# The last three chunks of an MLP weight brought by four loads of 32 partitions with an outermost dimension of eight

## The chip, the cores and the metric

The kernel runs on one core of one Trainium2 chip. The metric is the device time of one execution in microseconds (us). Three runs of the kernel before took 393.94, 395.52 and 395.59 us; their median is 395.52 us. One more execution was profiled, and all views of the profile are of that one.

## The reference, cut to what matters

A decode step for a batch of 8, one token each, in float32: adaptive layer norm, attention over the last 2048 rows of a cache of 8 key/value heads, and an MLP with squared ReLU. The lines that this case touches are the MLP's:

```python
mod = (_silu(c) @ w_mod).reshape(c.shape[0], 6, 1, -1)
sa, ca, ga, sb, cb, gb = (mod[:, i] for i in range(6))
x = x + ga * attention(layernorm(x) * (1 + ca) + sa, k_cache, v_cache, wq, wo)
h = layernorm(x) * (1 + cb) + sb
h = h @ w1 + b1                    # 512 -> 1792
r = jnp.where(h > 0, h, 0)
out = (r * r) @ w2 + b2            # 1792 -> 512
x = x + gb * out
```

## The kernel before, in words

Everything big is read once from HBM. Four SBUF slots of 4 MB (`slot0` to `slot3`, 128 partitions by 32 KB) take turns. `loads` is a list written out by hand: two halves of `w_mod`, two of `wq`, then key and value tiles of each batch element, two parts of `wo`, then `w1`, then `w2`. `pump()` issues the next loads as soon as a slot is free, all on SyncE's queue (SP); `done()` gives a slot back after its last matmul and pumps again. A large load has 128 partitions outermost, and its rows of HBM are split over the 16 DMA engines.

`w2` (1792 rows by 512) lies in its slot so that partition p holds rows 14p to 14p+13; "chunk" c (0 to 13) is row 14p+c of every partition, 256 KB over the 128 partitions. Before, `load` (L71 to L99) brings the chunks by four loads: 0 to 7, 8 to 11, 12, and 13. Since a later load on SP takes the semaphore of the one eight loads earlier, it is issued only after that one has landed.

The tail of the kernel is a chain. Matmuls with `wo` (L453) follow the two last `wo` loads; their output is added up (L463 to L471), normed, scaled and turned (`h2T`), and multiplied by `w1` (L485). ScalarE takes the ReLU into `r` (L493), VectorE squares it (L494). `r` has 128 partitions (four groups of 32, one per quarter of the 1792 hidden columns; the batch of 8 lies in the first rows of each group) by 448 columns. `to_columns` (L142, called at L496) turns 32x32 blocks of `r` into `rT`, 128 partitions by 14 chunks by 32, so that partition p of chunk c holds hidden column 14p+c. The 14 chunks are then multiplied by the chunks of `w2` in order (L505): four matmuls for each chunk, one per quarter of the output, each of which appears twice in the trace (112 entries). Two VectorE operations (L513, L514) make the output `y`, which SP stores (L515).

Of the kernel before, what the change touches and what calls it, by code (L numbers as in the profile page):

```python
# [18 lines left out]
def tile_adaln_cached_attention_mlp(  # L19
# [14 lines left out]
    nc = tc.nc  # L34
    P = 128
    B, HKV, SK, DH = k_cache.shape
    D = wq.shape[0]
# [33 lines left out]
    def load(key):  # L71
        s = free.pop(0)
        t = slots[s]
        held[key] = s
        kind = key[0]
        if kind in "KV":

            src = k_cache if kind == "K" else v_cache
            v = src[key[1], 4 * key[2] : 4 * key[2] + 4, SK - W :, :]
            v = v.rearrange("x (i j) d -> i x (j d)", i=32)  # L80
            nc.sync.dma_start(t, v)
            return
        if kind == "mod":
            pieces = [(0, w_mod.rearrange(r_kc, p=P)[:, 2 * key[1] : 2 * key[1] + 2])]
        elif kind == "wq":
            pieces = [(0, wq.rearrange(r_kc, p=P)[:, 2 * key[1] : 2 * key[1] + 2])]
        elif kind == "wo":
            v = wo.rearrange("(p i) n -> p i n", p=P)
            cuts = ((0, 16),) if key[1] == 0 else ((16, 28), (28, 32))
            pieces = [(lo - 16 * key[1], v[:, lo:hi]) for lo, hi in cuts]  # L90
        elif kind == "w1":
            v = w1.rearrange(r_kc, p=P)
            pieces = [(0, v[:, :2]), (2, v[:, 2:])]
        else:
            v = w2.rearrange("(p c) n -> p c n", p=P)
            pieces = [(lo, v[:, lo:hi]) for lo, hi in ((0, 8), (8, 12), (12, 13), (13, 14))]
        for lo, v in pieces:
            a, n = v.shape[1:]
            nc.sync.dma_start(t[:, lo * n : (lo + a) * n].rearrange("p (a n) -> p a n", n=n), v)  # L99

    def slot(key, n):
        t = slots[held[key]]
        return t[:, : t.shape[1] // n * n].rearrange("p (a n) -> p a n", n=n)
# [11 lines left out]
    def pump():  # L115
        while at[0] < len(loads) and free:
            load(loads[at[0]])
            at[0] += 1
# [22 lines left out]
    def to_columns(t, dest):  # L141
        nc.vector.transpose(dest, t.rearrange("p (l c) -> p c l", l=32))  # L142
# [349 lines left out]
    r = work.tile([P, FG], F32, name="relu", tag="a")  # L492
    nc.scalar.activation(r, ph[:, :FG], AF.Relu)  # L493
    nc.vector.tensor_mul(r, r, r)  # L494
    rT = work.tile([P, FC, 32], F32, name="rT", bufs=1)
    to_columns(r, rT)  # L496

    py = ps_t.tile([P, 512], F32, name="t_ps")
    for q in range(NQ):
# [52 lines left out]
```

## Time and profile before

| what | value |
|---|---|
| median of three runs | 395.52 us |
| the profiled execution's own time | 395.58 us |
| its span, first to last instruction | 393.7 us |
| PE / DVE / ACT busy, share of the span | 66% / 54% / 11% |
| 16 DMA engines, mean rate over the span | 419 GB/s |
| last `w2` matmul group (L505) | 112 entries, 4.9 us |
| `rT` transpose before it | 1 operation, 942 ns |

The profile is of one execution. Its own time, 395.58 us, is 1.9 us above the span, which counts only from the first to the last instruction. Most of the span is bound by the transfers (the DMA row of the 40 slices stands at 9 tenths from the second slice to the last but one); the change sits in the last 10 us.

### The profile page before, as it was taken

The numbers are of one execution on the slowest core, as the hardware profiler recorded it, in microseconds if no ns is written. First come the engines' busy times: TensorE is split into PE (matmuls) and PEld (weight loads), VectorE is DVE, ScalarE is ACT, GpSimd is POOL, SyncE is SP. The second block draws the span as 40 slices with busy tenths as digits, with TensorE's granted clock in tenths as the row PEclk, the third lists the DMA queues.
The fourth block names the chain that finished last, engine by engine and source line by source line (L and its number), as shares of the span: only waits on it lengthen the run. The fifth ranks groups of instructions, "written<-read, shape, count | busy, mean of one in ns | idle before, by whom it ended". The sixth has DMA issues, their size and how long they took to land.

```text
span 393.7 us, 4788 instructions
## 1 busy us (share of the span) xinstructions
PE 258.6 (66%) x2128; PEld 114.7 (29%) x2128; DVE 213.5 (54%) x226; ACT 42.0 (11%) x87; POOL 4.7 (1%) x12
## 2 busy tenths in 40 slices
PE   0445808678966694949394939393949394884784
PEld 0211301151441343324232523142215231451124
DVE  2420299399394849284928491849284926320022
ACT  1300100030030012001200120012001200130010
POOL 4000000000000000000000000000000000000000
PEclk9986758969975986889777968896779588998968
DMA  8999999999999999999999999999999999999992
GB/s 330 430 429 431 443 433 429 436 429 426 424 429 431 433 431 436 433 428 428 429 429 424 439 429 439 429 421 433 431 433 428 434 426 431 433 428 426 415 421 109
DMA packets 6853, 165.15 MB, mean 419 GB/s; under 512 B 808, under 2 KB 1072, under 8 KB 1328
## 3 DMA queue, kind: packets, MB, share of 16 engines
q1 hardware_dynamic: 6624, 164.69, 97.7%
q8 instruction: 17, 0.28, 0.3%
q10 hardware_dynamic: 144, 0.13, 0.1%
q14 instruction: 4, 0.03, 0.0%
q0 software_dynamic: 64, 0.01, 0.0%
HBM read 164.77 MB, written 0.07 MB: 419 GB/s over the span
## 4 chain that ended last, share of the span: by engine, by line
DMA 52%; PE 23%; DVE 22%; ACT 1%; issue 1%; DVEq 0%; ACTq 0%
DMA slot<-in_A_k_cache_dram 43%; DVE slot L287 20%; PE s_ps L297 15%; DMA slot<-in_A_wo_dram 7%; DMA xc_in<-in_xc_dram 3%; PE m_ps L221 2%; PE t_ps L485 1%; PE t_ps L505 1%; PE s_ps L453 1%; PE o_ps L378 1%; PE t_ps L366 1%; DVE pT L367 0%; PE t_ps L480 0%; PE m_ps L167 0%; ACT sq L163 0%
## 5 line engine op out<-in xcount | busy, mean ns | idle before, releaser
L287 DVE STREAM_TRANSPOSE slot<-slot 128x2048 f32<-128x2048 f32 x64 | 144.0, 2283 | 43.5 <-DMA slot<-in_A_k_cache_dram 43.3
L297 PE MATMUL s_ps<-slot,qb 128*32 128x512 f32 x512 | 121.1, 1095 | 69.6 <-DVE slot L287 68.7
L297 PEld LDWEIGHTS s_ps<-slot,qb 128*32 128x32 f32 x512 | 23.3, 136 | 147.0 <-issue 80.2
L378 PE MATMUL o_ps<-slot,pT 128*32 128x256 f32 x1024 | 59.6, 380 | 1.0 <-DMA slot<-in_A_v_cache_dram 1.0
L378 PEld LDWEIGHTS o_ps<-slot,pT 128*32 128x32 f32 x1024 | 47.0, 112 | 27.6 <-issue 18.2
L366 PE MATMUL t_ps<-ident,prd 128*128 128x128 f32 x128 | 27.4, 376 | 16.7 <-ACT prd L356 9.8
L309 DVE STREAM_TRANSPOSE s<-s_ps 128x512 f32<-128x512 f32 x8 | 5.7, 717 | 54.2 <-PE s_ps L297 54.2
L366 PEld LDWEIGHTS t_ps<-ident,prd 128*128 128x128 f32 x128 | 20.6, 192 | 22.3 <-ACT prd L356 22.1
L356 ACT ACTIVATE prd<-pr,rz 128x512 f32<-128x512 f32 x32 | 20.5, 710 | 9.6 <-DVE rz L348 9.6
L332 ACT ACTIVATE pr<-s,nm 128x512 f32<-128x512 f32 x8 | 5.8, 722 | 142.6 <-DVE nm L326 142.6
L367 DVE TENSOR_TENSOR pT<-t_ps,m 128x512 f32<-128x512 f32 x32 | 20.2, 668 | 0.7 <-PE t_ps L366 0.6
L388 ACT COPY o_sb<-o_ps 128x256 f32<-128x256 f32 x16 | 5.8, 363 | 121.9 <-PE o_ps L378 121.9
L243 PE MATMUL t_ps<-slot,h1T 128*32 128x512 f32 x64 | 12.5, 950 | 9.4 <-DMA slot<-in_A_wq_dram 9.4
L453 PE MATMUL s_ps<-slot,oT 128*32 128x512 f32 x64 | 8.9, 704 | 7.1 <-DMA slot<-in_A_wo_dram 7.1
L255 DVE STREAM_TRANSPOSE qT<-t_ps 128x512 f32<-128x512 f32 x2 | 1.4, 716 | 19.1 <-PE t_ps L243 18.9
L274 DVE TENSOR_TENSOR qb<-qrep,block 128x512 f32<-128x512 f32 x8 | 8.8, 1097 | 2.2 <-ACT qrep L266 2.2
L158 PE MATMUL m_ps<-xsum,sel 128*128 128x1 f32 x2 | 0.6, 363 | 14.0 <-DVE xsum L181 14.0
L344 PE MATMUL m_ps<-z,same 128*128 128x1 f32 x16 | 3.3, 273 | 9.2 <-ACT pr L332 9.2
L463 DVE COPY at_i<-s_ps 128x256 f32<-128x256 f32 x1 | 0.4, 424 | 15.3 <-PE s_ps L453 15.3
L243 PEld LDWEIGHTS t_ps<-slot,h1T 128*32 128x32 f32 x64 | 2.9, 163 | 18.8 <-issue 13.3
L221 PE MATMUL m_ps<-slot,cT 128*32 128x384 f32 x64 | 7.5, 639 | 0.0
L404 DVE TENSOR_TENSOR og<-m_ps,m 128x128 f32<-128x128 f32 x8 | 2.2, 271 | 9.1 <-PE m_ps L396 9.1
(91 smaller groups left out, 96.2 us busy)
## 6 DMA issues: line engine op xcount, KB each, us to landing
slot<-in_A_k_cache_dram SPq DMA_DIRECT2D x16, 4096.0 KB, 22.0
slot<-in_A_v_cache_dram SPq DMA_DIRECT2D x16, 4096.0 KB, 25.9
slot<-in_A_wq_dram SPq DMA_DIRECT2D x2, 4096.0 KB, 31.9
slot<-in_w_mod_dram SPq DMA_DIRECT2D x2, 3072.0 KB, 14.0
slot<-in_A_wo_dram SPq DMA_DIRECT2D x1, 4096.0 KB, 22.7
slot<-in_B_w_dram SPq DMA_DIRECT2D x2, 1792.0 KB, 28.0
slot<-in_A_wo_dram SPq DMA_DIRECT2D x1, 3072.0 KB, 27.5
slot<-in_B_w_dram SPq DMA_DIRECT2D x1, 2048.0 KB, 31.1
```

Source lines behind the costliest of these rows:

```text
L221: nc.tensor.matmul(pm[i][32 * q : 32 * q + 32, : 3 * P].rearrange("p (m n) -> p m n", m=3), cT[:, kc, :], wm[:, 3 * i : 3 * i + 3, q, :], ...
L243: nc.tensor.matmul(pq[t][32 * x : 32 * x + 32, :], hT[:, kc, :], w[:, 2048 * t + 512 * x : 2048 * t + 512 * x + 512], start=(kc == 0), sto ...
L274: nc.vector.tensor_mul(qb[b % 2][:, :, :, :REP], qrep_b[:, :, None, :, b].to_broadcast([P, 32, 4, REP]), block[:, None, :, None].to_broadc ...
L287: nc.vector.transpose(k, k)
L297: nc.tensor.matmul(S_[b][32 * x : 32 * x + 32, :].rearrange("p (j i) -> p j i", i=8), q[:, n : n + 32], k[:, :, c, :, x], start=(t == 0 an ...
L332: nc.scalar.activation(pr.rearrange("p j (a i) -> p j a i", a=4), S2_.pop(b).rearrange("p (a j i) -> p j a i", a=4, i=8), AF.Exp, bias=NM_ ...
L356: nc.scalar.activation(d, pr[:, 4 * n : 4 * n + 4, :, None].to_broadcast([P, 4, 32, 4]), AF.Copy, scale=RZ_[b][0])
L366: nc.tensor.transpose(pp[:, P * i : P * i + P], d[:, i].rearrange("p i u -> p (i u)"), one)
L367: nc.vector.tensor_mul(PT_[b][:, n].rearrange("p q j (x r) -> p q (j x) r", r=REP), pp.rearrange("p (y q r) -> p q y r", y=16, r=REP), m16 ...
L378: nc.tensor.matmul(o[32 * (m % 4) : 32 * (m % 4) + 32].rearrange("p u d -> p (u d)"), PT_[b][:, n, 2 * q + t, 2 * u : 2 * u + 2, :].rearra ...
L388: nc.scalar.copy(O_[b][:, t], o)
L453: nc.tensor.matmul(wo_ps[32 * (i % 4) : 32 * (i % 4) + 32, :], oT[:, i, :], slot(("wo", i // 16), D)[:, i % 16, :], start=(i < 4), stop=(i ...
```

## The change

Chunks 0 to 7 stay one load. The second load is cut to chunks 8 to 10. Chunks 11, 12 and 13 come by four loads, one for each group of 32 partitions. Each takes 32 rows of the view `(p c) n`, three chunks (6 KB) from each, and walks them with an outermost dimension of eight (`o`), an inner one of four (`i`): its rows are 8i+o for o = 0..7 and i = 0..3, in that order, while the destination is 32 partitions in order. So partition 32g+4o+i now holds, for these three chunks, what belongs to row 32g+8i+o.

To match, `rT` is made by two transposes: one of chunks 0 to 10 in the old order, one of chunks 11 to 13 in which the columns of each block are taken in the new order. The matmuls are unchanged.

```diff
         else:
             v = w2.rearrange("(p c) n -> p c n", p=P)
-            pieces = [(lo, v[:, lo:hi]) for lo, hi in ((0, 8), (8, 12), (12, 13), (13, 14))]
+            pieces = [(lo, v[:, lo:hi]) for lo, hi in ((0, 8), (8, 11))]
+
+            late = [
+                v[32 * g : 32 * g + 32, 11:].rearrange("(i o) c n -> o i (c n)", o=8) for g in range(4)
+            ]
         for lo, v in pieces:
             a, n = v.shape[1:]
             nc.sync.dma_start(t[:, lo * n : (lo + a) * n].rearrange("p (a n) -> p a n", n=n), v)
+        if kind == "w2":
+            for g, v in enumerate(late):
+                nc.sync.dma_start(t[32 * g : 32 * g + 32, 11 * D : 14 * D], v)
...
     rT = work.tile([P, FC, 32], F32, name="rT", bufs=1)
-    to_columns(r, rT)
+    nc.vector.transpose(rT[:, :11], r.rearrange("p (l c) -> p c l", l=32)[:, :11])
+    nc.vector.transpose(
+        rT[:, 11:].rearrange("p c (o i) -> p c o i", i=4),
+        r.rearrange("p (i o c) -> p c o i", i=4, o=8)[:, 11:],
+    )
```

## The prediction

> **What bounds the kernel now.** I read the chain that ended last first, from 368 us on, because the change only touches what happens behind the `wo` loads.
>
> ```profile
> 368.95 0.04 issue
> 368.99 3.69 PE s_ps L453 x32
> ...
> 378.18 5.17 PE t_ps L485 x32
> ...
> 383.94 0.63 DVE relu L494
> ...
> 384.60 0.95 DVE rT L142
> 385.56 0.04 issue
> 385.60 4.93 PE t_ps L505 x112
> ...
> 390.55 0.30 DVE y L513
> ```
>
> Columns are start, length, and what ran. From 368.95 us, when a `wo` load has landed, to the output no transfer stands in the chain: it is matmuls and small vector work. `w2` is not among what it waits for. The waits in that stretch say the same:
>
> ```profile
> DVE y L513 <- PE t_ps L505: 5.0, 1, 5.0
> PE t_ps L505 <- DVE rT L142: 2.0, 1, 2.0
> ```
>
> The matmuls of L505 waited for the transpose `rT` alone. How near `w2` was to being waited for comes from the issues and their times to landing, one load at a time (issue start in the timeline; the last number of the DMA row is us to landing):
>
> ```profile
> 353.84 0.33 SPq L99 DMA_DIRECT2D slot<-in_B_w_dram  x1
> slot<-in_B_w_dram SPq DMA_DIRECT2D x1, 2048.0 KB, 31.1
> 354.70 0.33 SPq L99 DMA_DIRECT2D slot<-in_B_w_dram  x1
> slot<-in_B_w_dram SPq DMA_DIRECT2D x1, 1024.0 KB, 32.7
> 355.10 0.40 SPq L99 DMA_DIRECT2D slot<-in_B_w_dram  x1
> slot<-in_B_w_dram SPq DMA_DIRECT2D x1, 256.0 KB, 32.9
> 361.69 0.33 SPq L99 DMA_DIRECT2D slot<-in_B_w_dram  x1
> slot<-in_B_w_dram SPq DMA_DIRECT2D x1, 256.0 KB, 26.9
> ```
>
> So chunks 0 to 7 landed at 353.84 + 31.1 = 384.9, chunks 8 to 11 at 387.4, chunk 12 at 388.0 and chunk 13 at 388.6 us. The last three chunks' matmuls (24 entries, of which the window catches 22) start here:
>
> ```profile
> 389.65 0.82 PE L505 MATMUL t_ps<-slot,rT 128*32 128x128 f32 x22
> ```
>
> Chunk 11 starts at 389.65. Each chunk takes about 0.82 / 3 = 0.27 us or less there, so chunk 13 starts near 390.1, some 1.5 us after it landed. The transfers are covered by 1.5 us or more.
>
> How the 16 DMA engines end is seen in half microseconds (last two columns: mean busy share of the 16 engines, GB/s; the column before them is the granted clock):
>
> ```profile
> 385.00:385.50 0.50, 0.00 (x0) 0.00 (x0) 0.50 (x1) 0.00 (x0) 0.00 (x0) 1.00 0.61 250
> 385.50:386.00 0.50, 0.40 (x8) 0.39 (x12) 0.04 (x1) 0.00 (x0) 0.00 (x0) 0.55 0.57 238
> 386.00:386.50 0.50, 0.50 (x20) 0.45 (x14) 0.00 (x0) 0.00 (x0) 0.00 (x0) 0.50 0.52 209
> 386.50:387.00 0.50, 0.50 (x16) 0.47 (x12) 0.00 (x0) 0.00 (x0) 0.00 (x0) 0.50 0.47 180
> ...
> 388.00:388.50 0.50, 0.50 (x16) 0.47 (x12) 0.00 (x0) 0.00 (x0) 0.00 (x0) 0.50 0.02 8
> ```
>
> At 385.0 the share is already 0.61, and it stays near one half until 387: about seven or eight engines are through by 385 to 386.5, and eight work on until about 388.1. The queue ends in two halves some 2.5 to 3 us apart.
>
> **The change part by part.**
>
> *The loads.* Four loads become six. The three chunks cost a late engine (388.0 - 387.4) + (388.6 - 388.0) for chunks 12 and 13, and a quarter of the 8-to-11 load for chunk 11, (387.4 - 384.9) / 4: together 0.6 + 0.6 + 0.6 = 1.8 us. No row shows a load whose outermost dimension is eight, so how it spreads must be bounded. One end: over all 16 engines like every load here, and the last landing stays at 388.6. Other end: over eight engines alone, which then carry twice their former share, 1.8 us more, while the others end 1.8 us earlier. If the eight are the half that ends early, the latest of them is through by about 386.5 and lands 0.5 us behind (as 388.1 and 388.6 are apart), 387.0; with 1.8 that is 388.8, and the late half ends at 388.6 - 1.8 = 386.8. If they are the late half: 388.6 + 1.8 = 390.4. Chunk 11 now needs all four loads, since its matmuls read all 128 partitions, so the limit is chunk 11's start, 389.65. At 388.6 or 388.8 the cover is still 0.8 us or more and the cost is nothing; at 390.4 it is uncovered. I take nothing. The nearest row for a small load is the `b_in` pair of four partitions:
>
> ```profile
> b_in<-in_B_b_dram POOLq DMA_DIRECT2D x1, 7.0 KB, 7.1
> ```
>
> Followed packet by packet, most of the engines that carried it belong to the half that ends early; no view groups that, so it only moves my chance from one half to about two thirds. [...]
>
> *SP's queue.* Two more issues of 0.33 to 0.40 us each (rows above), and the second to fourth of the new loads wait for the semaphore of a load eight earlier. That is visible now:
>
> ```profile
> SPq L99 <- DMA slot<-in_A_wo_dram: 6.1, 1, 6.1
> SPq L515 <- DMA slot<-in_A_wo_dram: 6.9, 1, 6.9
> SPq L515 <- DVE y L514: 22.2, 1, 22.2
> ```
>
> The last `w2` load waited for the first `wo` load (issued 361.69), and the store after it for the second (368.95). After: the second new load is issued at about 361.7, the third at 369.0, the fourth after the last `wo` load, about 371.5, and the store waits for the first `w1` load. The fourth is still 13 us ahead of the end of the queue, where all engines have work, so it joins the end in its turn. Behind these waits on SP there is only the store, which has 22 us to wait for `y`. Cost nothing; if the cover were gone each wait would add its few us to the landing.
>
> *The transposes.* One operation becomes two. Prices by shape:
>
> ```profile
> L142 DVE STREAM_TRANSPOSE rT<-relu 128x448 f32<-128x448 f32 x1 | 0.9, 942 | 0.0
> L142 DVE STREAM_TRANSPOSE h2T<-h_sb 128x128 f32<-128x128 f32 x1 | 0.4, 403 | 0.0
> ```
>
> The line through both is (942 - 403) / 320 = 1.68 ns an element. The first, 352 elements, takes 942 - 96 x 1.68 = 780 ns, 0.16 us less than now; the second, 96 elements, 403 - 32 x 1.68 = 349 ns, bounded by 0.2 and by 0.94 us if its split order is slow. Even then it ends near 386.4, three microseconds before chunk 11. What matters is whether chunk 0 waits for the first alone. Where a tile is made by two operations here (`at_i`), its reader waits for the part it reads:
>
> ```profile
> 373.18 0.14 PEld L467 LDWEIGHTS m_ps<-at_i,sel 128*32 128x32 f32 x4 [1.45 <-DVE at_i L463]
> 373.58 0.14 PEld L467 LDWEIGHTS m_ps<-at_i,sel 128*32 128x32 f32 x4 [0.26 <-ACT at_i L464]
> ```
>
> So L505 begins 0.16 us earlier, at 385.44. If it waited for both: 349 - 162 + some 20 ns of issue = 0.2 us later.
>
> *What 0.16 us earlier is worth.* The clock by its own steps (columns: us, PE busy, then the others; granted clock third from the right):
>
> ```profile
> 365.06:368.48 3.42, 1.96 (x20) 0.41 (x12) 0.00 (x0) 0.00 (x0) 0.00 (x0) 1.00 0.95 399
> 368.48:371.89 3.41, 2.90 (x28) 0.92 (x32) 0.00 (x0) 0.00 (x0) 0.00 (x0) 1.00 1.05 443
> 371.89:375.30 3.41, 1.92 (x18) 0.58 (x10) 1.11 (x5) 0.37 (x1) 0.00 (x0) 1.00 1.02 433
> 375.30:378.72 3.42, 2.77 (x14) 0.90 (x18) 1.56 (x6) 0.76 (x3) 0.00 (x0) 0.50 0.98 416
> 382.13:385.54 3.41, 1.51 (x20) 0.27 (x12) 1.56 (x2) 0.54 (x1) 0.00 (x0) 1.00 0.89 365
> 385.54:388.95 3.41, 3.35 (x64) 3.11 (x68) 0.01 (x1) 0.00 (x0) 0.00 (x0) 0.50 0.33 130
> 388.95:392.36 3.41, 1.52 (x56) 1.25 (x48) 0.58 (x2) 0.00 (x0) 0.00 (x0) 1.00 0.09 24
> ```
>
> L505 runs at half clock until 388.95 and at full clock after. Starting at 385.44, 0.10 us of the gain lies at full clock and 0.06 at half; at full-clock worth the end moves 0.10 + 0.06 / 2 = 0.13, about 0.14 us.
>
> *PE's waits.* Chunk 11 waits on five semaphores instead of two. The nearest row is the start of L505 now, which with its own waits comes 0.04 us behind the transpose (385.56 to 385.60 in the chain). Between 0 (the waits are passed while the array works off what is queued) and five times 0.04, 0.2 us; I take 0, since for all of L505's later chunks the chain shows one unbroken piece of 112 although they too have waits.
>
> Sum: -0.14 + 0 + 0 + 0. The profiled execution would be 395.58 - 0.14 = 395.44; it stands 0.06 above the median of the three runs, so 395.4 us.
>
> **The rivals.**
>
> *The eight are the late half (slower).* Place: the landing of the four loads. It decides once they land after chunk 11's new start, 389.65 - 0.14 = 389.5. At 390.4 chunk 11 waits 0.9 us and the end moves by that much instead of -0.14: 396.3. For it: eight engines are late, and nothing in a view names them. Against: the `b_in` loads.
>
> *Both transposes are waited for.* +0.2 instead of -0.14: about 395.7. Against it the `at_i` rows.
>
> *The clock goes another way (faster).* If 385.54 to 388.95 were granted full, the 3.35 us of work there would take 1.7. Chunk 11 would come at about 387.9, and then the landing would bound it: at 388.8 the gain is 389.65 - 388.8 = 0.8, 394.7; with a landing at 387 the whole 1.6, 393.9. For it: one of the three runs took 393.94. Against it: a step with 1.92 us of PE work was followed by half clock, one with 1.96 by full, and this step would have 1.51 + 0.10 = 1.61. [...]
>
> *The loads spread over all 16 after all.* Then the change does not do what its shape suggests, and the time is again 395.4.
>
> **How the numbers follow.** No wait on `w2`, with either spread: 0.60, 395.4. Late half: 0.22, 396.3. Both transposes: 0.06, 395.7. Clock: 0.12, 393.9 to 394.7. The range 393.9 to 396.6 holds all of these, with 0.3 above the late half for the 0.2 of PE's waits; the likeliest alone would be 395.1 to 395.7. Half a percent, 2 us, is about what a measurement of this kernel can tell from no change: below 393.5 needs the clock case with a little more than its 1.6 (0.08 of its 0.12 is generous), above 397.5 the late half with twice its price (0.07 of its 0.22). The rest, 0.85, is within.
>
> **What would show it.** Right: two `rT` transposes of near 0.78 and 0.35 us, L505 starting about 0.85 us after the square ends (now 385.60 - 384.58, about 1.0), and no wait of L505 on `in_B_w_dram`; the DMA share in the last us before the end either higher for longer and then falling at once (early half loaded), or eight engines at 0.5 until 390 (late half). Wrong: a wait `L505 <- DMA slot<-in_B_w_dram`, or a granted clock of 1.00 in the stretch after 385.5.

## The result, and the profile after

The changed kernel takes 396.73 us (median of six runs, 396.55 to 397.59), the kernel before 395.44 us (median of six, 393.94 to 395.81). The ratio is 1.0043, with a 95% interval of 1.0027 to 1.0060: slower by 0.4%, 0.13 us above the upper end of the range that the prediction gave. The profiled execution took 397.32 us and has a span of 394.8 us, against 393.7 before. Over the six runs the time outside the span varies from 1.8 to 2.9 us, so the readings below go by the span.

The chain that ended last, from 340 us on (start, length, what ran). Before, no transfer stood in it behind the `wo` loads; now one of `w2` does:

```profile
342.40 28.61 DMA slot<-in_A_wo_dram
371.01 0.02 issue
371.02 19.28 DMA slot<-in_B_w_dram
390.31 0.14 issue
390.44 0.90 PE t_ps L516 x24
```

The fourth new load, issued at 371.02, landed at 390.31, and the last 24 matmul entries (chunks 11 to 13; L516 is the former L505) waited for it. The timeline around it:

```profile
384.11 0.78 DVE L503 STREAM_TRANSPOSE rT<-relu 128x352 f32<-128x352 f32 x1
384.81 0.30 DVE L504 STREAM_TRANSPOSE rT<-relu 128x96 f32<-128x96 f32 x1
...
384.94 4.27 PE L516 MATMUL t_ps<-slot,rT 128*32 128x128 f32 x88 [1.79 <-DVE rT L503]
...
390.44 0.86 PE L516 MATMUL t_ps<-slot,rT 128*32 128x128 f32 x24 [1.23 <-DMA slot<-in_B_w_dram]
391.36 0.29 DVE L524 TENSOR_TENSOR y<-t_ps,mod 128x128 f32<-128x128 f32 x1 [6.25 <-PE t_ps L516]
...
392.01 0.35 SPq L526 DMA_DIRECT2D out_dram<-y  x1
```

The 88 entries of chunks 0 to 10 are one piece that starts when the first transpose ends; then PE idles 1.23 us. The end of the queue, in half microseconds (last three columns: granted clock, busy share of the 16 engines, GB/s):

```profile
385.00:385.50 0.50, 0.50 (x12) 0.49 (x16) 0.11 (x1) 0.00 (x0) 0.00 (x0) 0.50 0.89 356
385.50:386.00 0.50, 0.50 (x17) 0.49 (x13) 0.00 (x0) 0.00 (x0) 0.00 (x0) 0.50 0.70 184
...
387.50:388.00 0.50, 0.50 (x18) 0.49 (x12) 0.00 (x0) 0.00 (x0) 0.00 (x0) 0.50 0.18 74
388.00:388.50 0.50, 0.50 (x19) 0.49 (x14) 0.00 (x0) 0.00 (x0) 0.00 (x0) 0.60 0.18 74
388.50:389.00 0.50, 0.50 (x28) 0.44 (x18) 0.00 (x0) 0.00 (x0) 0.00 (x0) 1.00 0.15 61
389.00:389.50 0.50, 0.21 (x8) 0.00 (x0) 0.00 (x0) 0.00 (x0) 0.00 (x0) 1.00 0.12 49
```

From 387.5 on the share is 0.18: of 16 engines, three are at work (0.18 x 16 = 2.9), each at 74 / 3 = 25 GB/s, about a sixteenth of the 416 that all engines move together at a share of 0.98 (before, 375.30 to 378.72 us). Before, eight worked on until 387.5 (share 0.50). So neither half alone carries the four loads: most of their engines are through by 387.5, three go on to 389, two of them (0.12 x 16 = 1.9) to 389.5 or later.

Between the two profiles: the `wo` loads landed 0.4 us earlier in this execution (PE resumes at 368.57 instead of 368.99); the transpose gives 0.2; so L516 starts 0.66 us earlier. The wait takes 1.23, and the group, now in two pieces of 4.27 and 0.86 us instead of one of 4.88, takes 0.25 more. That makes -0.66 + 1.23 + 0.25 = 0.8, which is how much later `y` starts (391.36 instead of 390.55). The span is 1.1 longer; the rest, 0.25 us, lies behind the store: from its issue to the end of the span it is 2.50 us before (391.19 to 393.69) and 2.75 after (392.01 to 394.76).

### The profile page after: what moved, and what is told of

It reads as the page before. It is cut to its first block, busy times and chain, and to the rows that moved or that the text cites. A ratio compares the mean times of both kernels' runs of the same rounds, so it can differ in the third digit from the quotient of the medians.

```text
span 394.8 us, 4792 instructions
## 1 busy us (share of the span) xinstructions
PE 256.8 (65%) x2128; PEld 113.2 (29%) x2128; DVE 213.6 (54%) x227; ACT 41.9 (11%) x87; POOL 4.7 (1%) x12
## 4 chain that ended last, share of the span: by engine, by line
DMA 58%; DVE 22%; PE 19%; issue 0%; ACT 0%; DVEq 0%; ACTq 0%
DMA slot<-in_A_k_cache_dram 43%; DVE slot L294 20%; PE s_ps L304 15%; DMA slot<-in_A_wo_dram 7%; DMA slot<-in_B_w_dram 5%; DMA xc_in<-in_xc_dram 3%; PE m_ps L228 2%; PE o_ps L385 1%; PE t_ps L373 1%; DVE pT L374 0%; DVE e_sb L155 0%; PE t_ps L516 0%; ACT prd L363 0%; DVE s L316 0%; DVE s L320 0%
## 5 line engine op out<-in xcount | busy, mean ns | idle before, releaser
L373 PE MATMUL t_ps<-ident,prd 128*128 128x128 f32 x128 | 26.1, 361 | 16.7 <-ACT prd L363 9.5
L373 PEld LDWEIGHTS t_ps<-ident,prd 128*128 128x128 f32 x128 | 19.6, 184 | 22.2 <-ACT prd L363 21.7
L516 PE MATMUL t_ps<-slot,rT 128*32 128x128 f32 x112 | 5.1, 358 | 3.0 <-DVE rT L503 1.8
```

Of the source, the lines that this page charges most:

```text
L373: nc.tensor.transpose(pp[:, P * i : P * i + P], d[:, i].rearrange("p i u -> p (i u)"), one)
```

## The experiments

Two theories stood against each other first, and a third beside them. Theory 1: the new loads run on eight engines, some of them engines that end late, and those now carry double. Theory 2: the second to fourth load are issued too late, behind semaphores of older loads. Theory 3: loads of 32 partitions are slow by themselves. Unless said otherwise, the kernels differ from the kernel before or the changed one only by the lines shown, and the ratio is to the kernel before in runs beside them.

**The transpose alone**

```diff
-    to_columns(r, rT)
+    for lo, hi in ((0, 11), (11, FC)):
+        nc.vector.transpose(rT[:, lo:hi], r.rearrange("p (l c) -> p c l", l=32)[:, lo:hi])
```

> The loads of before, and only the transpose cut in two (chunks 0 to 10, then 11 to 13, columns in the old order). Both theories: no wait on w2, the last matmul group starts 0.16 to 0.2 us earlier, the time falls by 0.1 to 0.2 us. If the first matmul waited for both transposes it would rise by about 0.2 us.

Ratio 0.9998, interval 0.9982 to 1.0015: no change that twelve runs can tell, which includes the expected 0.1 to 0.2 us. The profile shows the step: L506 starts 0.83 us after the first piece of the transpose began (384.68 to 385.51), where before it was 1.00 us (384.60 to 385.60).

```profile
384.68 1.00 DVE L497 STREAM_TRANSPOSE rT<-relu 128x352 f32<-128x352 f32 x2
...
385.51 4.93 PE L506 MATMUL t_ps<-slot,rT 128*32 128x128 f32 x112 [1.79 <-DVE rT L497]
```

So the transposes are not what slowed the changed kernel; the loads are.

**Four loads of 32 partitions, rows in order**

```diff
-                v[32 * g : 32 * g + 32, 11:].rearrange("(i o) c n -> o i (c n)", o=8) for g in range(4)
+                v[32 * g : 32 * g + 32, 11:].rearrange("p c n -> p (c n)") for g in range(4)
```

> The same six loads of w2 as the changed kernel (four of 32 partitions, issued behind the same semaphores), but rows in natural order, so the outermost dimension is 32 and not eight; the transpose is cut in two in the old order. Theory 1 (the latest of the eight engines carries double): no wait on w2 at the end, time 395.2 to 395.6 (0.2 gained by the transpose, 0.25 lost because the store's semaphore is checked earlier in the final row of checks). Theory 2 (the second to fourth load are issued too late, behind older loads) or theory 3 (loads of 32 partitions are slow by themselves): the wait of about 1.2 us stays, 396.5 or more.

398.23 us, ratio 1.0088 (1.0065 to 1.0112): slower still. Theory 1's number missed; the time lies where theories 2 and 3 had it, but not in the way they said, for chunk 0 already waits for its load, which is ahead of the four:

```profile
386.20 4.28 PE L513 MATMUL t_ps<-slot,rT 128*32 128x128 f32 x88 [2.25 <-DMA slot<-in_B_w_dram]
...
391.06 0.86 PE L513 MATMUL t_ps<-slot,rT 128*32 128x128 f32 x24 [0.58 <-DMA slot<-in_B_w_dram]
```

The windows show why:

```profile
374.00:375.00 1.00, 0.27 (x2) 0.30 (x2) 0.55 (x3) 0.00 (x0) 0.00 (x0) 1.00 0.98 416
...
385.00:385.50 0.50, 0.00 (x0) 0.00 (x0) 0.50 (x1) 0.00 (x0) 0.00 (x0) 1.00 1.02 221
385.50:386.00 0.50, 0.00 (x0) 0.00 (x0) 0.42 (x2) 0.00 (x0) 0.00 (x0) 1.00 0.82 184
```

At 374 us all engines busy means 416 GB/s; at 385, in these loads, all engines busy means 221. The engines are occupied and move half as much, which is called crowding from here on. So this run can't decide on theory 1's double load, and it raises the question of what crowds.

It does show on how many engines the four loads run. In the traces a load leaves one packet under 512 B on each engine that it uses: the 46 transfers on SP's queue in the kernel before leave 736 of 4 bytes, 16 each. The changed kernel and this run differ only in the order of rows in the four loads (and in the second transpose):

```profile
DMA packets 6724, 165.13 MB, mean 418 GB/s; under 512 B 808, under 2 KB 1072, under 8 KB 1328
...
DMA packets 6756, 165.13 MB, mean 418 GB/s; under 512 B 840, under 2 KB 1104, under 8 KB 1360
```

The first line is the changed kernel's, the second this run's. It has 32 small packets more, eight for each of the four loads: 16 engines here, eight in the changed kernel. The kernel before has 808 too, for four loads on 16 engines leave as many as two on 16 and four on eight.

**One load with an outermost dimension of eight**

```diff
-            late = [... for g in range(4)]
+            late = v[:, 11:].rearrange("(i o) c n -> o i (c n)", o=8)
...
-            for g, v in enumerate(late):
-                nc.sync.dma_start(t[32 * g : 32 * g + 32, 11 * D : 14 * D], v)
+            nc.sync.dma_start(t[:, 11 * D : 14 * D], late)
```

> Chunks 11 to 13 by one load of 128 partitions whose outermost dimension is eight, issued without the three waits; the order of rows is then not the one that the transposes make, so the output is not the reference's. Theory 1: the wait for w2 stays at 1.0 to 1.4 us, time 396.2 to 396.8. Theories 2 and 3: no wait, 395.2 to 395.6.

398.00 us, ratio 1.0093 (1.0071 to 1.0115); the rows lie in another order than the transposes make, so this run tells of times alone. The wait is there although the load is issued once and early, so theories 2 and 3 are not needed for it; but it is longer than theory 1 had said. The first line is the wait of chunk 0, the second that of chunk 11 for the load on eight engines:

```profile
385.80 4.92 PE L513 MATMUL t_ps<-slot,rT 128*32 128x128 f32 x88 [3.21 <-DMA slot<-in_B_w_dram]
...
392.10 1.51 PE L513 MATMUL t_ps<-slot,rT 128*32 128x128 f32 x24 [1.38 <-DMA slot<-in_B_w_dram]
```

Even chunk 0, whose load lies ahead in the queue, came 0.9 us later than in the changed kernel (384.94). In this run too the engines were busy without moving much: 197 GB/s at a share of 0.93.

```profile
385.00:385.50 0.50, 0.00 (x0) 0.00 (x0) 0.00 (x0) 0.00 (x0) 0.00 (x0) 0.50 0.93 197
...
390.00:390.50 0.50, 0.50 (x16) 0.26 (x7) 0.00 (x0) 0.00 (x0) 0.00 (x0) 0.50 0.18 74
```

And again three engines are left over at the end (0.18 x 16 = 2.9).

**One chunk instead of three on the eight**

```diff
-            pieces = [(lo, v[:, lo:hi]) for lo, hi in ((0, 8), (8, 11))]
+            pieces = [(lo, v[:, lo:hi]) for lo, hi in ((0, 8), (8, 13))]
...  (and 11 becomes 13 in the late loads and in the transposes)
```

> Only chunk 13 by the four loads with an outermost dimension of eight, chunks 8 to 12 by one load of 128 partitions. Theory 1: the latest engine carries 0.6 us more instead of 1.8, landing about 389.1, chunk 13 is due about 389.9, so no wait; time 395.2 to 395.7. Theory 2: the fourth load is issued as late as in the changed kernel, so a wait of the same size stays, 396.5. Theory 3: each load is a third as long, wait 0.4 us or less.

395.46 us, ratio 1.0016 (1.0003 to 1.0029). No wait for chunk 13: all 112 entries are one piece. The four loads were issued between 355 and 372 us as in the changed kernel, so theory 2 falls here; theory 3 would have allowed this too.

```profile
385.14 4.93 PE L516 MATMUL t_ps<-slot,rT 128*32 128x128 f32 x112 [1.90 <-DVE rT L503]
```

**Two chunks on the eight** (11 becomes 12 in the same lines)

> Chunks 12 and 13 by the four loads with an outermost dimension of eight. Theory 1: the last landing lies between that of one chunk (388.9) and of three chunks (390.3), about 389.6, which is when chunk 12 is due, so a wait of 0 to 0.4 us and a time between the two, 395.6 to 396.4. Rival (the semaphore waits in front of the second to fourth load decide): they are issued at the same times as in the changed kernel, so the landing is 390.3 again and the time 396.5 or more.

396.61 us, ratio 1.0043 (1.0025 to 1.0060): as slow as three chunks, above the 395.6 to 396.4 expected. Chunk 12 waited until 390.35 in the profile, not 389.6. Both numbers are those of the rival. But with one chunk the same times of issue gave no wait, and here the engines do not stand idle for want of an issue: the rates at 385.5 to 387 are again low for high shares:

```profile
385.50:386.00 0.50, 0.50 (x28) 0.50 (x23) 0.00 (x0) 0.00 (x0) 0.00 (x0) 1.00 0.85 180
386.00:386.50 0.50, 0.50 (x22) 0.28 (x12) 0.00 (x0) 0.00 (x0) 0.00 (x0) 1.00 0.73 156
...
390.35 1.08 PE L516 MATMUL t_ps<-slot,rT 128*32 128x128 f32 x16 [1.25 <-DMA slot<-in_B_w_dram]
```

180 GB/s at 0.85 is half of what 416 at 0.98 would give (360). So a second cost rides on theory 1, the crowding. By share and rate an 8 KB row, as in chunks 8 to 11, takes an engine 0.31 us at 416 GB/s and 0.98, and 0.61 to 0.63 in these windows from 385.5 to 387 (the third is 115 GB/s at 0.55). That the uneven steps from one to two to three chunks come from this alone is likely, not shown.

**One load of 128 partitions over all 16 engines**

```diff
-            pieces = [(lo, v[:, lo:hi]) for lo, hi in ((0, 8), (8, 12), (12, 13), (13, 14))]
+            pieces = [(lo, v[:, lo:hi]) for lo, hi in ((0, 8), (8, 11), (11, 14))]
...  (and the transpose cut at 11, columns in the old order)
```

> Chunks 11 to 13 by one load of 128 partitions in natural order, over all 16 engines, and the transpose cut in two at chunk 11: the 32-partition loads and the outermost dimension of eight are both gone. Theory 1 (the latest of the eight engines carries double): no wait on w2 at the end, last landing 388.3 to 388.7, time 394.6 to 395.5. Rival (one load less of lead, or chunk 11 needing all of a 768 KB load, is what costs): the wait on w2 stays at over 0.5 us, 396 or more.

394.95 us, ratio 0.9999 (0.9986 to 1.0012). The wait is gone. The same three chunks in one load landed at 354.68 + 33.4 = 388.1, a little before the 388.3 expected:

```profile
354.68 0.34 SPq L99 DMA_DIRECT2D slot<-in_B_w_dram  x1
slot<-in_B_w_dram SPq DMA_DIRECT2D x1, 768.0 KB, 33.4
...
384.48 4.96 PE t_ps L506 x112
```

So in the median neither the larger last load nor the earlier need for it costs; what costs is what the four loads do, which land 390.31 - 388.1 = 2.2 us later. On eight engines each carries eight rows more of 6 KB, and in the trace of the changed kernel such a row takes an engine 0.234 us (median of those that start before 385 us): 8 x 0.234 = 1.9 us. The other 0.3 to 0.4 us are put down to crowding. This split is worked out; no run had the eight engines without the crowding.

What the median hides: none of these twelve runs took less than 394.2 us, while five of the 24 of the kernel before beside them took 393.6 to 393.9. When the tail runs fast, the earlier need for chunk 11 may cost up to half a microsecond; these runs are too few to settle it.

**Which engines are late**

The kernel before, with four tiny loads behind `w2`, of 8, 4, 2 and 17 rows of 64 bytes. GpSimd copies them in the order 17, 2, 4, 8.

> The kernel before, and behind the loads of w2 four tiny loads of 64 bytes a row with 8, 4, 2 and 17 rows, which GpSimd copies in the order 17, 2, 4, 8 rows when they have landed; each lands when its last engine has worked through its queue. If the engines that these loads use are all of the half that ends early, all four copies start at about 384.9 to 386.9; if all of the late half, all at 387.5 or later; if the loads mix the halves, the copies step from early to late, and the row number at the step tells where a late engine lies. The time itself does not change by more than 0.3 us.

```profile
385.88 0.48 POOL L518 COPY seen<-probe 17x16 f32<-17x16 f32 x2 [380.06 <-DMA probe<-in_B_w_dram]
387.26 0.19 POOL L518 COPY seen<-probe 4x16 f32<-4x16 f32 x1 [0.91 <-DMA probe<-in_B_w_dram]
388.13 0.19 POOL L518 COPY seen<-probe 8x16 f32<-8x16 f32 x1 [0.69 <-DMA probe<-in_B_w_dram]
```

The loads of 17 and of 2 rows were there at about 386 (two copies in one entry), the one of 4 rows at 387.26, the one of 8 rows at 388.13. The load of 4 rows touched an engine over a microsecond later than those of the loads of 17 and 2 rows, and the load of 8 rows one of the last of all, for in this run's own windows the share falls to nothing between 387.5 and 388:

```profile
387.50:388.00 0.50, 0.50 (x20) 0.50 (x14) 0.00 (x0) 0.00 (x0) 0.00 (x0) 0.50 0.09 33
388.00:388.50 0.50, 0.50 (x16) 0.50 (x12) 0.00 (x0) 0.00 (x0) 0.19 (x1) 0.50 0.00 0
```

In the changed kernel, too, three engines are left over (share 0.18 from 387.5 on) and the other five are through: the eight are a mixture of early and late. Which engines a load of 8, 4, 2 or 17 rows takes was not shown, for no view numbers them; measured is the order of the copies alone.

**Cutting the transpose where it pays**

The kernel before with its own loads, and the transpose cut at chunk 4 instead of 11 (the diff of the first experiment with 4 for 11).

> The kernel before with its own loads, and the transpose cut at chunk 4 instead of done in one: the first piece is 128x128 and takes 0.40 us where the whole takes 0.94. The last matmul group starts 0.5 us earlier; the end moves by 0.3 to 0.5 us where nothing else is waited for, a ratio of 0.9988 to 0.9992. If the second piece were waited for, or the landing of chunk 13 (388.6) became the bound, the gain is under 0.2 us.

393.85 us, ratio 0.9973 (0.9962 to 0.9984): faster than both kernels, and by more than twice what was expected, 1.06 us. In the profile the matmuls start when the load of chunks 0 to 7 has landed, and then wait for the next ones; the transfers are now the bound:

```profile
385.03 1.96 PE L506 MATMUL t_ps<-slot,rT 128*32 128x128 f32 x64 [2.49 <-DMA slot<-in_B_w_dram]
...
387.39 1.70 PE L506 MATMUL t_ps<-slot,rT 128*32 128x128 f32 x48 [0.41 <-DMA slot<-in_B_w_dram]
```

Its eleven runs lie within 0.42 us (393.67 to 394.09), the 24 runs of the kernel before beside it within 2.24 (393.63 to 395.87), with the same lower end. The kernel before sometimes reaches this time and often not. In the profile here the granted clock was 1.00 in every microsecond from 385 to 389; in the one before it was 0.50 from 386 to 388.5. An earlier start does not keep the clock up by itself: in the profile of the next run the matmuls start at 384.54, and the clock is 0.50 until 387.5. What decides it was not tested.

**The same cut in the changed kernel**

```diff
-    nc.vector.transpose(rT[:, :11], r.rearrange("p (l c) -> p c l", l=32)[:, :11])
+    for lo, hi in ((0, 4), (4, 11)):
+        nc.vector.transpose(rT[:, lo:hi], r.rearrange("p (l c) -> p c l", l=32)[:, lo:hi])
```

> The changed kernel, with its first transpose (chunks 0 to 10) cut again at chunk 4, the cut that made the kernel before faster by 1.06 us. Theory 1 (the end hangs on the landing of the four loads): the matmuls start 0.4 us earlier and wait 0.4 us longer or more, and the time stays that of the changed kernel, 1.003 to 1.006 of before. Rival (the matmuls and the clock still set the end): it falls by 0.4 to 1.1 us, to 395.6 to 396.3.

397.03 us, ratio 1.0057 (1.0039 to 1.0074): no gain. The wait grew from 1.23 to 1.86 us and chunk 11 started at 390.55, as in the changed kernel (390.44). The landing sets the end.

```profile
384.54 4.14 PE L517 MATMUL t_ps<-slot,rT 128*32 128x128 f32 x88 [2.09 <-DVE rT L505]
...
390.55 0.86 PE L517 MATMUL t_ps<-slot,rT 128*32 128x128 f32 x24 [1.86 <-DMA slot<-in_B_w_dram]
```

**What crowds**

The kernel with four loads of 32 partitions in order, with other partitions in each load:

```diff
-                v[32 * g : 32 * g + 32, 11:].rearrange("p c n -> p (c n)") for g in range(4)
+                v[:, 11:].rearrange("(i g) c n -> g i (c n)", g=4)[g] for g in range(4)
...
-                nc.sync.dma_start(t[32 * g : 32 * g + 32, 11 * D : 14 * D], v)
+                nc.sync.dma_start(t[g::4, 11 * D : 14 * D], v)
```

> The run with four loads of 32 partitions in natural order, but each load takes every fourth partition (g, g+4, g+8, ...) instead of 32 in a row; number, size, issue and engines of the loads are the same. If many engines writing into few neighbouring partitions is what made that run slow (398.2 us, busy share 1.0 at 220 GB/s), the rate comes back to 380 GB/s or more at a share of 1.0, the wait for w2 at the end goes, and the time is 394.8 to 395.6. If loads of 32 partitions are slow by themselves, it stays at 397.5 or more.

394.79 us, ratio 0.9999 (0.9985 to 1.0013); 3.4 us faster than with 32 partitions in a row. All that has changed is which partitions share a load, and with them the rows that are read from HBM.

```profile
385.00:385.50 0.50, 0.50 (x28) 0.50 (x24) 0.00 (x0) 0.00 (x0) 0.00 (x0) 1.00 0.62 258
```

258 GB/s at a share of 0.62 is 416 at a full one, the rate at 374 us; in a row it was 221 at 1.02. Theory 3 falls: loads of 32 partitions are not slow by themselves, and with 32 neighbouring partitions in each, from 16 engines, the rate halved. The expected end of the wait did not come in this execution:

```profile
388.37 0.86 PE L513 MATMUL t_ps<-slot,rT 128*32 128x128 f32 x24 [1.08 <-DMA slot<-in_B_w_dram]
```

The clock was 1.00 throughout, the matmuls of chunks 0 to 10 were through by 387.3, and the landing at about 388.2, as early as over 16 engines (388.1), was then the bound. Why neighbouring partitions halve the rate was not shown; measured are the 221 with them and the return to 416 with every fourth partition.

## Why the prediction was wrong

**What bounds before: right.** The cover of `w2` was read as 1.5 us for chunk 13, and chunk 11 as due at 389.5. Removing the late landing (the load over 16 engines) brings the old time back. The sign of being wrong that the prediction named, a wait of these matmuls on `w2`, is what came: 1.23 us.

**The transposes: right.** 0.78 and 0.35 us were forecast, 0.78 and 0.30 measured; the first matmuls waited for the first piece alone; the gain was 0.2 us in the profile, too small for the runs to show.

**The loads: the step that failed.** The prediction put this term at nothing ("I take nothing"). One end of its bounds, "over eight engines alone", was what happened (eight small packets for each of the four loads, against 16 with the rows in order). But then it asked which half those were, the early or the late, and took the early one with two chances in three because small loads seemed to lie there. The rows that it leaned on, the `b_in` pair, were issued on GpSimd's queue, not on SP's, and nothing in the record says that the two choose alike. The eight are neither half. Three of them end late (the share of 0.18 after 387.5; the probes of 4 and 8 rows, too, were late, at 387.26 and 388.13), and one late engine among eight is enough: the fourth load landed with its last engine, at 390.31, and PE waited 1.23 us. Even a random pick of eight engines out of 16 of which eight were late would nearly always have held one.

The price of the case that came true was near: 390.4 forecast for a late engine that carries 1.8 us more, 390.31 measured. That it was so near is in part luck: this execution was 0.4 us ahead, and the 0.3 to 0.4 us put down to crowding made up for it. For the end, the recorded sentence says that it moves by the whole 0.9 us; its 396.3 is right with 0.9 - 0.14.

**A cost that the working did not have: crowding.** It counted a load's time as bytes by rate. In the changed kernel 184 GB/s ran at a share of 0.70 between 385.5 and 386, where 416 at 0.98 would give about 300; a row of 6 KB that starts in that half microsecond takes 0.40 us (median), against 0.234 before 385. The load of chunks 8 to 10 landed at 354.37 + 32.4 = 386.8 against 354.21 + 32.0 = 386.2 in the kernel with one load over 16 engines:

```profile
354.37 0.33 SPq L103 DMA_DIRECT2D slot<-in_B_w_dram  x1
slot<-in_B_w_dram SPq DMA_DIRECT2D x1, 768.0 KB, 32.4
```

```profile
354.21 0.33 SPq L99 DMA_DIRECT2D slot<-in_B_w_dram  x1
slot<-in_B_w_dram SPq DMA_DIRECT2D x1, 768.0 KB, 32.0
```

Of the 0.6 us, 0.2 are the execution's own (PE resumes behind a `wo` load that much apart); about 0.4 are left. That early engines write there where late ones still write, and that this is the same crowding as with neighbouring partitions, is the author's estimate and was not shown.

**PE's waits: right.** From the landing to chunk 11's first matmul the chain has 0.14 us, and it has the same 0.14 in the kernel with one load over 16 engines, from the landing of chunks 0 to 7 (384.35) to chunk 0's first matmul. Waiting for four loads instead of one cost nothing that the chains show.

**SP's queue: "cost nothing" was off by 0.25 us.** The waits in front of the loads did cost nothing (one chunk on the eight, issued as late, has no wait). But SP ends the kernel with a row of checks on the semaphores of its loads, 0.06 us each, and the number of loads before the store decides where the store's own check stands in that row. In the traces two checks stand behind it with four `w2` loads, three with three and five with six; and the check itself passes 1.55 us after the store's issue before and 1.61 after. From the store's issue to the end of the span it is 2.50 us with four `w2` loads (before, and with the cut at 4), 2.57 with three, and 2.75 with six (changed kernel; with every fourth partition 2.74). This term explains most of the 0.4 us by which 396.3, the forecast for the late half, was still short, and with it why even the upper end of the range was passed.

**The clock rival** was about the kernel before more than about the change. The granted clock was 0.50 from 385 to 388 in the changed kernel's profile too. The spans of its six runs are 394.7 to 394.8: the landing fixes them. Those of before vary from 391.8 to 394.1 in the runs beside the experiments, and the profile that the sum was made on, 393.7, is near the upper end; so the sum started from one of the slower executions.

## What to carry to other kernels

A load on eight engines landed here with the latest of them: the share was 0.18 from 387.5 on, three engines, and the landing came at 390.31. The count of packets under 512 B told on how many engines the loads ran (808 against 840). Before steering bytes onto the "early" engines find out which those are: a few tiny loads of different row counts at the end of the queue, each copied by an idle engine, showed in one run that they end at different times (385.88, 387.26 and 388.13 us). A cover of 1.5 us for the last transfer was cover for a tail that ran at a slow clock (0.50 from 386 to 388.5 us); it was also all that a faster tail could gain, as the cut at chunk 4 showed (1.06 us), which starts the consumer on a small first piece and then hangs on the landing. Read the busy share of the transfers beside their rate: here a full share at half the rate (221 GB/s at 1.02, against 416 at 0.98) was crowding, not bandwidth, and which partitions share a load, with the rows that go with them, made it and removed it (258 at 0.62).

## What the runs showed of the hardware that was not expected

The engines end in an uneven way that repeats: in the kernel before, and in all variants without eight-engine loads but the crowded one, about eight of 16 are at work until 387 to 387.5 us, and the others are through two to three us earlier:

```profile
387.00:387.50 0.50, 0.50 (x16) 0.47 (x12) 0.00 (x0) 0.00 (x0) 0.00 (x0) 0.50 0.50 193
...
q8 instruction: 17, 0.28, 0.3%
```

The second line is the fetching of instructions, which takes time of the same 16 engines. 0.3% of 16 engines' 393.7 us is 19 us; on eight of them that is 2.4 us each, about the distance between the halves. The packets in the trace of the kernel before bear it out. A load's small last packet on each engine tells when that engine was through (chunk 13's last one ends at 388.22 us, and the load has landed at 388.64). For the loads that end at 10 to 27 us, ahead of the first fetch, the 16 engines lie within 0.83 us. A fetch is one packet of 16 KB and about 1.0 us on one engine. After the first, one engine ends 1.9 us behind the earliest, the others still within 0.83. With the ninth, an engine that was already behind goes to 3.3. At 348 us, after 14 fetches, eight engines lie 2.2 to 3.7 us behind the earliest and the other eight within 1.5. Followed packet by packet, the late half are the engines that the fetches went through, about eight of them, in two rounds; no run without the fetches was made.

Six-KB rows from 16 engines into 32 partitions in a row moved at 221 GB/s with all engines busy (share 1.02), and at 258 GB/s with a share of 0.62, 416 for a full one, when the same loads went to every fourth partition.
